# Bias columns, a softmax scaling and two steps of a weight split move to other engines and other places in the queues

## The chip, the cores and the metric

One core of one Trainium2 chip runs the whole program. The metric is device time in microseconds (us); smaller is better. The kernel before took 667.5 us (median of 665.89, 667.50 and 667.67).

## What is computed

An attention block is followed by two gated feed-forward layers, all in 32-bit floats.

```
scores = q @ k.T / 8 + bias      # 2 batches x 8 heads, 576 x 576, head size 64
bias   = relu(x @ w1 + b1) @ w2  # x from the positions alone; 32 hidden units -> 8 heads
attn   = exp(scores - max); attn /= attn.sum() + 1e-9
x      = (attn @ v) as 1152 tokens x 512
x      = (sigmoid(x @ w_gate) * (x @ w_val)) @ w_out           # layer 0, 1536 hidden
xn     = x / rms(x) * g
out    = (silu(xn @ w_gate) * (xn @ w_val)) @ w_out            # layer 1, 1536 hidden
```

## The kernel before, in words

TensorE's fast format holds fewer bits than a 32-bit float, so the feed-forward operands are each a high word plus a low word, and every product is three matmuls. The weights lie in memory as 64-bit floats (two 32-bit words). A *piece* is one 128x512 block of them (72 pieces: 2 layers x 12 hidden blocks x gate, value and output weights). A piece is loaded into one of three buffers `wr` (`piece_load`) and made into a 32-bit float and then into the two words by four steps (`piece_step`), of which the last two are alike in both kernels:

- step 0 masks and shifts the upper word (VectorE, into `tt`);
- step 1 takes the absolute value of the upper word (ScalarE, `ab`), merges sign and shifted bits (VectorE, `ff`), scales the lower word to an integer (ScalarE, `rb`) and adds the two (GpSimd, `ff`);
- step 2 sets tiny values to zero (VectorE, `ab`) and rounds to the high word (ScalarE, `wh` or `wv`);
- step 3 subtracts to get the low word (VectorE, `wl` or `wv`).

The order of every engine's queue is the order in which the program issues, so each engine works strictly through its own list. `advance` deals out piece steps one at a time, in a fixed cycle over the four steps, wherever `ready` allows the next piece to take that step. `fetch` issues the load of a piece two ahead of the count of first merges done (`done[1]`).

The attention part runs in 40 *turns* (one batch, one pair of heads, one block of 128 or 64 query rows each). Each turn issues, in an order written out by hand (`ORDERS`): M0/M1, score plus bias and its minimum (VectorE); X0/X1, exponentials with sums (ScalarE); N, the sums of the turn before inverted (VectorE) and its two 128x576 exponentials scaled (`normal`); T, transposes on TensorE of the block three turns back, and E0 to E2, their copies out of PSUM; Q, the scores of the next turn; P and V, the products with v; and A and b, up to two steps of the bias table (`bias_step`). A bias step builds four 128-wide column tiles `ht` for a new group of 16 positions (`bias_h`), multiplies those of the group before (`bias_mm`, results `be`), and mirrors and stores the one before that (`bias_end`). The first 16 of 36 groups are done before turn 0; groups 16 to 25 fall to turns 0 to 4, two in each; groups 26 to 35 to turns 8 to 17. `BIAS_H` names, for each group, the columns that ScalarE and GpSimd build; VectorE builds the others.

The feed-forward part is 72 steps `s`: a block of 384 tokens times one hidden block. At each, `gate_val(s)` issues 24 matmuls and the gating (ScalarE `sg`, VectorE `g`, ScalarE `gh`), `low_part(s)` the gated rows' low word `gl` (VectorE), and `out_mm(s-2)` the 12 matmuls of the output product of two steps earlier. Output products of two to four hidden blocks gather in a pair of PSUM tiles `acc`; at the last of them (`closing`) the sums are read out into `part` (VectorE, in part ScalarE), and the next group's first matmul may only then overwrite them. Steps of pieces are dealt out between these in two halves, as many as `pace` says (5 to 8).

Of the kernel before, what the change touches and what calls it, by code (L numbers as in the profile page):

```python
# [8 lines left out]
F32 = mybir.dt.float32  # L9
F32R = mybir.dt.float32r  # L10
U32 = mybir.dt.uint32
I32 = mybir.dt.int32
AF = mybir.ActivationFunctionType
ALU = mybir.AluOpType
# [20 lines left out]


BIAS_H = {k: ((), (2, 3) if k % 2 else (3,)) for k in range(16)}
BIAS_H |= {k: ((), (3,)) for k in range(16, 36)}

BIAS_HALF_DVE = (0, 1, 2, 3)  # L40
PRE = 16
# [33 lines left out]
def fused_kernel(ctx: ExitStack, tc: tile.TileContext, qk, vp, tab, pcol, invp, prm, wts, rg, out):  # L75
    nc = tc.nc
# [11 lines left out]
    def bank2(nm):  # L88
        return ps2.tile([128, 2, 512], F32, tag="two", name=nm)
# [206 lines left out]
    def jobs(n):  # L296
        return 1 if UNITS[n][2] == 4 else 2
# [56 lines left out]
    def normal(n):  # L354
        p, sm = st[n, "p"]
        k = jobs(n)
        nc.vector.tensor_scalar(sm[:, :k], sm[:, :k], 1e-9, None, op0=ALU.add)
        rs = w2.tile([128, 2], F32, tag="rs", name=f"rs{n}", bufs=3)
        nc.vector.reciprocal(rs[:, :k], sm[:, :k])  # L359
        for j in range(k):  # L360
            nc.gpsimd.tensor_scalar(p[:, j], p[:, j], rs[:, j : j + 1], 1.0, op0=ALU.mult, op1=ALU.mult)  # L361

    pts = {}

# [63 lines left out]
    def members(l, g):  # L428
        a = sum(GROUPS[l][:g])
        return range(a, a + GROUPS[l][g])  # L430
# [7 lines left out]
    NS = len(STEPS)  # L438
# [5 lines left out]
    wraw = {}  # L444
    mid = {}
# [21 lines left out]
    def piece_step(k, i):  # L467
        mc = pools["mc"]
        if i == 0:
            tt = mc.tile([128, 512], U32, tag="tt", name=f"tt{k}")  # L470
            nc.vector.tensor_scalar(  # L471
                tt, wraw[k][:, :, 1], 3, 0x3FFFFFFF, op0=ALU.logical_shift_left, op1=ALU.bitwise_and
            )
            mid[k] = tt
        elif i == 1:
            raw = wraw.pop(k)
            lw, hw = raw[:, :, 0], raw[:, :, 1]
            tt = mid[k]
            ab = mc.tile([128, 512], F32, tag="ab", name=f"ab{k}", bufs=3)
            nc.scalar.activation(ab, hw.bitcast(F32), AF.Abs)  # L480
            ff = mc.tile([128, 512], U32, tag="ff", name=f"ff{k}", bufs=2)
            nc.vector.scalar_tensor_tensor(ff, hw, 0xC0000000, tt, op0=ALU.bitwise_and, op1=ALU.bitwise_or)  # L482
            rb = mc.tile([128, 512], I32, tag="rb", name=f"rb{k}")
            nc.scalar.activation(rb, lw, AF.Copy, scale=2.0**-29)  # L484
            nc.gpsimd.tensor_tensor(ff.bitcast(I32), ff.bitcast(I32), rb, op=ALU.add)  # L485
            mid[k] = (ab, ff)
        elif i == 2:
            ab, ff = mid[k]
            nc.vector.scalar_tensor_tensor(ab, ab, TINY_HI, ff.bitcast(F32), op0=ALU.is_ge, op1=ALU.mult)  # L489
            nc.scalar.activation(ring[k % RING][0], ab, AF.Copy)  # L490
        else:
            ab, _ = mid.pop(k)
            hi, lo = ring[k % RING]
            nc.vector.tensor_tensor(lo, ab, hi.bitcast(F32), op=ALU.subtract)
            wp[PIECES[k]] = (hi, lo)
# [24 lines left out]
    def low_part(s):  # L520
        gh, g32 = gt[s]
        gl = pools["me"].tile([128, CH], F32R, tag="gl", name=f"gl{s}", bufs=3)
        nc.vector.tensor_tensor(gl, g32, gh.bitcast(F32), op=ALU.subtract)  # L523
        gt[s] = (gh, gl)

    def out_mm(s):
        l, g, c, f = STEPS[s]
        gh, gl = gt.pop(s)
        oh, ol = wp[l, f, 2]
        head, last = f == members(l, g)[0], f == members(l, g)[-1]  # L530
        final = g == len(GROUPS[l]) - 1
        if head:
            acc[c] = (bank2(f"acc{l}{g}{c}a"), bank2(f"acc{l}{g}{c}b"))
        a = acc[c]
        cs = slice(c * CH, c * CH + CH)
        def product(m):
            dst = a[m % 2][:, m // 2, :CH]
            for k, (st_, mv) in enumerate(((oh, gh), (oh, gl), (ol, gh))):
                nc.tensor.matmul(
                    dst, st_[:, m * 128 : m * 128 + 128], mv, start=(head and k == 0), stop=(last and k == 2)  # L540
                )

        def collect(m):
            dst = a[m % 2][:, m // 2, :CH]
            pt = part[m][:, cs]
            if g > 0:
                nc.vector.tensor_tensor(pt, dst, pt, op=ALU.add)  # L547
            elif m % 2:
                nc.vector.tensor_copy(pt, dst)
            else:  # L550
                nc.scalar.activation(pt, dst, AF.Copy)
            if final and l == 1:
                (nc.sync if m % 2 == 0 else nc.scalar).dma_start(out[m * 128 : m * 128 + 128, cs], pt)


        for m in range(NCC):
            product(m)
            if s == NS - 1:
                collect(m)
        if not last:  # L560
            return
        if s < NS - 1:
            for m in range(NCC):
                collect(m)
        if final and l == 0:
            norm_queue.append([s + 2, c, 0, None])
# [52 lines left out]
    done = [0, 0, 0, 0]  # L619
    loaded = [0]  # L620
    phase = [0]

    def released(k):
        return USES[PIECES[k][:2]][-1] + 3
# [4 lines left out]
    def closing(s):  # L629
        return 0 <= s < NS - 1 and STEPS[s][:3] != STEPS[s + 1][:3]  # L630


    def pace(s):
        need, begun = 5, done[0] + done[1] + done[2] - 3 * done[3]
        for k in range(done[3], min(NPC, done[3] + RING)):
            todo = 4 * (k + 1 - done[3]) - begun
            need = max(need, -(-todo // max(1, deadline(k) - s - 1)))
        return min(need, 8)

    def ready(i):  # L640
        k = done[i]
        if k >= (NPC if i == 0 else done[i - 1]):
            return False
        if i == 0:
            return k < loaded[0] and done[1] >= k
        if i == 1:
            return done[2] >= k - 1 and done[3] >= k - 2
        return i == 3 or k < room[0]
# [5 lines left out]
    def fetch():  # L654
        while loaded[0] < NPC and done[1] >= loaded[0] - 2:
            piece_load(loaded[0])
            loaded[0] += 1

    def advance(limit, micro):
        room[0] = limit  # L660
        idle = 0
        while micro and idle < 4:
            fetch()
            i = (2, 1, 0, 3)[phase[0]]
            phase[0] = (phase[0] + 1) % 4
            if ready(i):
                piece_step(done[i], i)
                done[i] += 1
                micro -= 1
                idle = 0  # L670
            else:
                idle += 1
# [18 lines left out]
    for n in range(NU + TL + 1):  # L691
# [13 lines left out]
        def load_new():  # L705
# [16 lines left out]
            "E1": lambda: evac(1),  # L722
            "E2": lambda: evac(2),
            "N": lambda: 0 <= n - 1 < NU and normal(n - 1),
            "C": lambda: n >= NBIAS + LAG and advance(EARLY if live else EARLY + MORE, 1 if live else 2),
            "B": lambda: live and feed_bias(n + 4),
            "A": lambda: nb > 1 and bias_step(),
# [24 lines left out]
    for s in range(EARLY + MORE, RING):  # L752
        tag, size = ("pt", 9 * 128) if s < EARLY + MORE + 2 else ("v", 1024)
# [5 lines left out]
    for s in range(NS + 2):  # L759
        while s < NS and (STEPS[s][0], STEPS[s][3], 1) not in wp:  # L760
            advance(done[3] + 1, 1)
        if 0 < s < NS:
            gate_val(s)
        micro = pace(s)
        if any(q[0] <= s for q in norm_queue):
            micro = min(micro, 2)

        parts = (0, micro) if closing(s - 2) else (micro // 2, micro - micro // 2)
        for half in range(2):
            k = done[3]  # L770
            if k < NPC:
                lim = k
                while lim < NPC and lim < k + 3 and (lim < RING or released(lim - RING) <= s):
                    lim += 1
                advance(lim, parts[half])
            if half == 0:
                if s < NS:
                    low_part(s)
                if s > 1:
                    l, _, _, f = STEPS[s - 2]  # L780
                    while (l, f, 2) not in wp:
                        advance(done[3] + 1, 1)
                    out_mm(s - 2)
                while norm_queue and norm_queue[0][0] <= s:
                    _, c, stage, box = norm_queue.pop(0)
                    norm_stage(c, stage, box)
                    if stage < 3:
                        norm_queue.append([s + 1, c, stage + 1, box])
# [68 lines left out]
```

## Time and profile before

| | us |
|---|---|
| median of three runs | 667.5 |
| the profiled execution's own time | 664.12 |
| its span, first to last instruction | 662.3 |
| TensorE busy | 643.4 (97%) |
| VectorE busy | 454.8 (69%) |
| ScalarE busy | 348.6 (53%) |
| GpSimd busy | 211.6 (32%) |

The profile names engines PE (TensorE matmul), PEld (its weight loads), DVE (VectorE), ACT (ScalarE), POOL (GpSimd) and SP (the queue that issues most DMAs); L12 is line 12 of the kernel. TensorE's granted clock was 0.999 of full speed on average. Turn 0 begins at 28.43 us of the span, and the first feed-forward matmul is at 189.06 us.

### The profile page before, as it was taken

The numbers are of one execution on the slowest core, as the hardware profiler recorded it, in microseconds if no ns is written. First come the engines' busy times: TensorE is split into PE (matmuls) and PEld (weight loads), VectorE is DVE, ScalarE is ACT, GpSimd is POOL, SyncE is SP. The second block draws the span as 40 slices with busy tenths as digits, with TensorE's granted clock in tenths as the row PEclk, the third lists the DMA queues.
The fourth block names the chain that finished last, engine by engine and source line by source line (L and its number), as shares of the span: only waits on it lengthen the run. The fifth ranks groups of instructions, "written<-read, shape, count | busy, mean of one in ns | idle before, by whom it ended". The sixth has DMA issues, their size and how long they took to land.

```text
span 662.3 us, 11825 instructions
## 1 busy us (share of the span) xinstructions
PE 643.4 (97%) x4454; PEld 575.6 (87%) x4454; DVE 454.8 (69%) x968; ACT 348.6 (53%) x743; POOL 211.6 (32%) x259
## 2 busy tenths in 40 slices
PE   8889999999999899999999999999999999999997
PEld 4236666777679899999999999999999999999997
DVE  6997898688656667867677678788777777321322
ACT  4648889798685555444444564553555545211110
POOL 6566677476453322222222221110223223000000
PEclk9999999999999999999999999999999999999999
DMA  8866855663124333323233332111234330000111
GB/s 212 276 234 191 226 185 184 232 215 98 50 66 127 104 120 95 96 97 102 93 112 108 96 95 65 64 55 42 84 108 117 98 105 33 1 0 1 48 48 48
DMA packets 28088, 71.73 MB, mean 108 GB/s; under 512 B 3456, under 2 KB 6528, under 8 KB 28032
## 3 DMA queue, kind: packets, MB, share of 16 engines
q1 hardware_dynamic: 27168, 69.80, 34.2%
q10 hardware_dynamic: 864, 1.18, 0.5%
q8 instruction: 35, 0.57, 0.3%
q14 instruction: 21, 0.17, 0.1%
HBM read 57.72 MB, written 13.25 MB: 107 GB/s over the span
## 4 chain that ended last, share of the span: by engine, by line
PE 61%; DVE 13%; ACT 12%; issue 5%; POOL 5%; POOLq 0%; DVEq 0%
PE gv L509 26%; PE s L310 6%; PE pv L399 6%; PE tp L379 6%; POOL ff L485 4%; DVE ab L489 4%; ACT ab L480 3%; ACT rb L484 3%; PE bps L211 3%; DVE part L547 2%; DVE g L515 2%; ACT sg L513 2%; ACT gh L517 1%; ACT wh L490 1%; DVE tt L471 1%
## 5 line engine op out<-in xcount | busy, mean ns | idle before, releaser
L485 POOL TENSOR_TENSOR ff<-ff,rb 128x512 int32<-128x512 int32 x72 | 96.5, 1341 | 284.5 <-ACT rb L484 216.2
L515 DVE TENSOR_TENSOR g<-gv,sg 128x384 f32<-128x384 f32 x72 | 40.1, 558 | 112.5 <-PE gv L509 66.7
L517 ACT ACTIVATE gh<-g 128x384 fp32r<-128x384 f32 x72 | 37.9, 526 | 76.4 <-DVE g L515 76.4
L509 PE MATMUL gv<-nh,wv 128*128 128x384 f32 x288 | 76.5, 337 | 0.0
L509 PE MATMUL gv<-xh,wh 128*128 128x384 f32 x216 | 73.2, 339 | 0.0
L509 PE MATMUL gv<-xl,wh 128*128 128x384 f32 x216 | 72.9, 337 | 0.0
L509 PE MATMUL gv<-xh,wl 128*128 128x384 f32 x216 | 72.9, 337 | 0.0
L489 DVE SCALAR_TENSOR_TENSOR ab<-ab,ff 128x512 f32<-128x512 f32 x72 | 49.9, 693 | 28.7 <-POOL ff L485 28.7
L361 POOL TENSOR_SCALAR p<-p,rs 128x576 f32<-128x576 f32 x72 | 60.4, 847 | 13.4 <-DVE rs L359 13.1
L490 ACT ACTIVATE wh<-ab 128x512 fp32r<-128x512 f32 x42 | 26.5, 631 | 66.9 <-DVE ab L489 66.8
L328 DVE CUSTOM_DVE_ANT_0 t<-s,bt 128x576 f32<-128x576 f32 x72 | 51.8, 751 | 13.8 <-PE s L310 12.3
L193 DVE TENSOR_SCALAR ht<-w1l,bpc 128x304 f32<-128x304 f32 (+17 forms) x100 | 58.8, 652 | 0.0
L513 ACT ACTIVATE sg<-gv 128x384 f32<-128x384 f32 x72 | 34.5, 479 | 44.9 <-PE gv L509 44.8
L349 ACT ACTIVATE p<-t,mn 128x576 f32<-128x576 f32 x72 | 55.2, 767 | 3.4 <-DVE mn L328 3.3
L310 PE MATMUL s<-raw 64*128 64x288 f32 (+1 forms) x320 | 52.6, 427 | 4.6 <-issue 3.1
L399 PEld LDWEIGHTS pv<-pt,v 128*64 128x64 f32 (+1 forms) x800 | 40.2, 136 | 16.8 <-ACT pt L703 10.2
L523 DVE TENSOR_TENSOR gl<-g,gh 128x384 fp32r<-128x384 f32 x72 | 40.1, 557 | 18.6 <-ACT gh L517 18.6
L509 PEld LDWEIGHTS gv<-nh,wv 128*128 128x128 f32 x288 | 52.4, 188 | 0.0
L399 PE MATMUL pv<-pt,v 128*64 128x128 f32 (+2 forms) x800 | 49.6, 268 | 1.0 <-ACT pt L703 1.0
L490 ACT ACTIVATE wv<-ab 128x512 fp32r<-128x512 f32 x30 | 19.0, 633 | 57.5 <-DVE ab L489 57.4
L482 DVE SCALAR_TENSOR_TENSOR ff<-wr,tt 128x512 uint32<-128x512 uint32 x72 | 49.2, 683 | 0.0
L509 PE MATMUL gv<-nh,wh 128*128 128x384 f32 x144 | 48.7, 338 | 0.0
(356 smaller groups left out, 1588.6 us busy)
## 6 DMA issues: line engine op xcount, KB each, us to landing
wr<-wts SPq DMA_DIRECT2D x72, 512.0 KB, 3.6
bias_d<-be SPq DMA_DIRECT2D x36, 295.5 KB, 3.8
bt<-bias_d SPq DMA_DIRECT2D x16, 576.0 KB, 4.8
raw<-qk SPq DMA_DIRECT2D x16, 288.0 KB, 6.3
v<-vp SPq DMA_DIRECT2D x8, 320.0 KB, 3.6
v<-vp SPq DMA_DIRECT2D x8, 160.0 KB, 4.8
bt<-bias_d SPq DMA_DIRECT2D x8, 144.0 KB, 3.2
out<-part SPq DMA_DIRECT2D x6, 192.0 KB, 1.8
```

Source lines behind the costliest of these rows:

```text
L193: nc.vector.tensor_scalar(ht, src, bpc[:, t : t + 1], 0.0, op0=ALU.add, op1=ALU.max)
L310: nc.tensor.matmul(dst, raw[r, 0, it * 128 : it * 128 + rows_of(it)], raw[r, 1, hf * 288 : hf * 288 + 288], start=True, stop=True,)
L328: nc.vector.tensor_tensor_reduce(t, sp[:, :, :288], bt[:, j].rearrange("p (a c) -> p a c", a=2), -SCALE, 3.0e38, ALU.add, ALU.min, mn[:, j ...
L349: nc.scalar.activation(p[:, j], t.rearrange("p a c -> p (a c)"), AF.Exp, bias=mn[:, j : j + 1], scale=-1.0, accum_out=sm[:, j : j + 1],)
L361: nc.gpsimd.tensor_scalar(p[:, j], p[:, j], rs[:, j : j + 1], 1.0, op0=ALU.mult, op1=ALU.mult)
L399: nc.tensor.matmul(box["ps"][j * 64 : j * 64 + 64, :n], v[:k, 2 * j if it == 4 else j, c, :], pt[:k, c, j * 64 : j * 64 + 64] if it == 4 e ...
L482: nc.vector.scalar_tensor_tensor(ff, hw, 0xC0000000, tt, op0=ALU.bitwise_and, op1=ALU.bitwise_or)
L485: nc.gpsimd.tensor_tensor(ff.bitcast(I32), ff.bitcast(I32), rb, op=ALU.add)
L489: nc.vector.scalar_tensor_tensor(ab, ab, TINY_HI, ff.bitcast(F32), op0=ALU.is_ge, op1=ALU.mult)
L490: nc.scalar.activation(ring[k % RING][0], ab, AF.Copy)
L509: nc.tensor.matmul(ps[:, :CH], wt[:, cs], xt[:, cc, :], start=(k == 0), stop=(k == 11))
L515: nc.vector.tensor_tensor(g32, pss[1][:, :CH], sg, op=ALU.mult)
```

## The change

Four edits:

1. Of bias groups 16 to 25, column 1 is built by ScalarE (Relu with a bias) in place of VectorE, and column 3 by VectorE in place of GpSimd.
2. The scaling of the exponentials of turns 0 to 5 is issued to VectorE in place of GpSimd.
3. In a piece, step 0 now holds the shift (VectorE, straight into `ff`), the absolute value and the scaling of the lower word (both ScalarE, the latter in place into `wr`); step 1 is left with the merge (VectorE, in place) and the add (GpSimd, which reads the lower word from `wr`, every second 32-bit word). The dealing cycle is 0, 2, 1, 3 in place of 2, 1, 0, 3, and step 0 may run one piece ahead of step 1.
4. Where `out_mm(s-2)` closes an accumulation, `low_part(s)` is issued behind it, that is behind the reads of the sums.

```diff
 BIAS_H = {k: ((), (2, 3) if k % 2 else (3,)) for k in range(16)}
-BIAS_H |= {k: ((), (3,)) for k in range(16, 36)}
+BIAS_H |= {k: ((1,), ()) if k < 26 else ((), (3,)) for k in range(16, 36)}
+NORM_DVE = range(6)
...
         for j in range(k):
-            nc.gpsimd.tensor_scalar(p[:, j], p[:, j], rs[:, j : j + 1], 1.0, op0=ALU.mult, op1=ALU.mult)
+            if n in NORM_DVE:
+                nc.vector.tensor_scalar(p[:, j], p[:, j], rs[:, j : j + 1], None, op0=ALU.mult)
+            else:
+                nc.gpsimd.tensor_scalar(p[:, j], p[:, j], rs[:, j : j + 1], 1.0, op0=ALU.mult, op1=ALU.mult)
...
         if i == 0:
-            tt = mc.tile([128, 512], U32, tag="tt", name=f"tt{k}")
-            nc.vector.tensor_scalar(
-                tt, wraw[k][:, :, 1], 3, 0x3FFFFFFF, op0=ALU.logical_shift_left, op1=ALU.bitwise_and
-            )
-            mid[k] = tt
+            raw = wraw[k]
+            lw, hw = raw[:, :, 0], raw[:, :, 1]
+            ff = mc.tile([128, 512], U32, tag="ff", name=f"ff{k}", bufs=3)
+            nc.vector.tensor_scalar(ff, hw, 3, 0x3FFFFFFF, op0=ALU.logical_shift_left, op1=ALU.bitwise_and)
+            ab = mc.tile([128, 512], F32, tag="ab", name=f"ab{k}", bufs=3)
+            nc.scalar.activation(ab, hw.bitcast(F32), AF.Abs)
+            nc.scalar.activation(lw.bitcast(I32), lw, AF.Copy, scale=2.0**-29)
+            mid[k] = (ab, ff)
         elif i == 1:
             raw = wraw.pop(k)
             lw, hw = raw[:, :, 0], raw[:, :, 1]
-            tt = mid[k]
-            ab = mc.tile([128, 512], F32, tag="ab", name=f"ab{k}", bufs=3)
-            nc.scalar.activation(ab, hw.bitcast(F32), AF.Abs)
-            ff = mc.tile([128, 512], U32, tag="ff", name=f"ff{k}", bufs=2)
-            nc.vector.scalar_tensor_tensor(ff, hw, 0xC0000000, tt, op0=ALU.bitwise_and, op1=ALU.bitwise_or)
-            rb = mc.tile([128, 512], I32, tag="rb", name=f"rb{k}")
-            nc.scalar.activation(rb, lw, AF.Copy, scale=2.0**-29)
-            nc.gpsimd.tensor_tensor(ff.bitcast(I32), ff.bitcast(I32), rb, op=ALU.add)
-            mid[k] = (ab, ff)
+            ab, ff = mid[k]
+            nc.vector.scalar_tensor_tensor(ff, hw, 0xC0000000, ff, op0=ALU.bitwise_and, op1=ALU.bitwise_or)
+            nc.gpsimd.tensor_tensor(ff.bitcast(I32), ff.bitcast(I32), lw.bitcast(I32), op=ALU.add)
...
         if i == 0:
-            return k < loaded[0] and done[1] >= k
+            return k < loaded[0] and done[1] >= k - 1 and done[2] >= k - 2 and done[3] >= k - 2
...
-            i = (2, 1, 0, 3)[phase[0]]
+            i = (0, 2, 1, 3)[phase[0]]
...
-                if s < NS:
+                if s < NS and not closing(s - 2):
                     low_part(s)
                 if s > 1:
...
                     out_mm(s - 2)
+                if closing(s - 2):
+                    low_part(s)
```

## Rows read from the trace of the kernel before

**Rows 1.** Window: us, then busy (instructions) of PE, PEld, DVE, ACT, POOL, clock, DMA

```profile
300.00:350.00 50.00, 47.41 (x270) 46.83 (x270) 35.70 (x64) 23.91 (x45) 12.11 (x9) 1.00 0.31 96
```

**Rows 2.** Waits of PE: waiting line, releaser, total us, times, longest us

```profile
PE acc001a L539 <- ACT part L551: 2.0, 1, 2.0
...
PE acc021a L539 <- DVE part L547: 1.3, 1, 1.3
PE acc020a L539 <- DVE part L547: 1.3, 1, 1.3
...
PE pv L399 <- ACT pt L703: 1.0, 2, 0.6
PE ss L587 <- DVE nrm L582: 0.9, 1, 0.9
```

**Rows 3.** Windows of turns 0 to 4, columns as in the first group

```profile
28.43:32.99 4.56, 3.13 (x24) 1.70 (x24) 4.49 (x12) 2.91 (x8) 0.00 (x0) 1.00 1.01 368
32.99:39.70 6.71, 4.52 (x40) 2.04 (x40) 6.14 (x15) 2.79 (x6) 4.14 (x6) 1.00 0.68 221
39.70:45.80 6.10, 5.10 (x35) 2.17 (x36) 5.53 (x15) 2.45 (x6) 3.91 (x6) 1.00 0.53 197
45.80:51.57 5.77, 5.77 (x35) 2.60 (x34) 5.74 (x15) 4.12 (x9) 3.77 (x7) 1.00 0.77 259
51.57:56.79 5.22, 5.22 (x52) 2.97 (x50) 5.12 (x15) 3.85 (x9) 2.88 (x5) 1.00 0.56 176
```

**Rows 4.** Timeline, turns 0 and 2: start, us, instruction, count [idle before <- releaser]

```profile
29.79 2.64 DVE L193 TENSOR_SCALAR ht<-w1l,bpc 128x576 f32<-128x576 f32 x6
...
41.33 1.67 DVE L193 TENSOR_SCALAR ht<-w1l,bpc 128x512 f32<-128x512 f32 x3
41.52 2.09 POOL L361 TENSOR_SCALAR p<-p,rs 128x576 f32<-128x576 f32 x2 [2.12 <-DVE rs L359]
...
43.53 0.55 DVE L220 TENSOR_SCALAR be<-bps,nip,corr 128x264 f32<-128x264 f32 x1 [0.53 <-PE bps L211]
```

**Rows 5.** Groups by line, 28.4 to 56.8 us: count, busy us, mean ns, idle before

```profile
L193 DVE TENSOR_SCALAR ht<-w1l,bpc 128x576 f32<-128x576 f32 (+9 forms) x30 | 17.3, 639 | 0.0
```

**Rows 6.** Groups by line of ACT, whole span

```profile
L349 ACT ACTIVATE p<-t,mn 128x576 f32<-128x576 f32 x72 | 55.2, 767 | 3.4 <-DVE mn L328 3.3
L480 ACT ACTIVATE ab<-wr 128x512 f32<-128x512 f32 x72 | 47.5, 660 | 0.0
L484 ACT ACTIVATE rb<-wr 128x512 int32<-128x512 uint32 x72 | 47.5, 660 | 0.0
...
L490 ACT ACTIVATE wh<-ab 128x512 fp32r<-128x512 f32 x42 | 26.5, 631 | 66.9 <-DVE ab L489 66.8
...
L513 ACT ACT_TABLE_LOAD x2 | 2.6, 1283 | 3.7 <-PE gv L509 3.7
L216 ACT ACT_TABLE_LOAD x1 | 1.3, 1283 | 6.3 <-DVE corr L678 6.3
```

**Rows 7.** Timeline, 302 to 306 us, around a closing

```profile
303.69 0.56 DVE L523 TENSOR_TENSOR gl<-g,gh 128x384 fp32r<-128x384 f32 x1 [0.59 <-ACT gh L517]
...
304.17 0.55 DVE L547 TENSOR_TENSOR part<-acc012a,part 128x384 f32<-128x384 f32 x1
...
305.79 0.41 PE L539 MATMUL acc020a<-gh,wv 128*128 128x384 f32 x1 [1.28 <-DVE part L547]
```

**Rows 8.** Timeline of POOL, 198 to 211 us: first and last of four adds

```profile
198.04 1.28 POOL L485 TENSOR_TENSOR ff<-ff,rb 128x512 int32<-128x512 int32 x1 [1.57 <-ACT rb L484]
...
210.04 1.29 POOL L485 TENSOR_TENSOR ff<-ff,rb 128x512 int32<-128x512 int32 x1 [2.60 <-ACT rb L484]
```

**Rows 9.** The page's groups by line: the other operations of a piece

```profile
L489 DVE SCALAR_TENSOR_TENSOR ab<-ab,ff 128x512 f32<-128x512 f32 x72 | 49.9, 693 | 28.7 <-POOL ff L485 28.7
...
L482 DVE SCALAR_TENSOR_TENSOR ff<-wr,tt 128x512 uint32<-128x512 uint32 x72 | 49.2, 683 | 0.0
```

**Rows 10.** The page's DMA issues: count, KB each, median us to landing

```profile
wr<-wts SPq DMA_DIRECT2D x72, 512.0 KB, 3.6
```

## The prediction

> **What bounds the kernel now.** I read the busy shares first, then the list of waits of TensorE (PE), then windows of the stages, then the timeline where PE idles. PE is busy 643.4 us of a span of 662.3, so only what stops PE can be won: about 19 us, of which the start-up takes a good part. In a mid feed-forward window PE is busy 47.41 of 50 us, with 270 matmuls at the spacing of about 0.174 us that the timeline shows for 384 columns (270 x 0.174 = 47.0), so little stall hides inside "busy" there; VectorE has 35.7, ScalarE 23.9, GpSimd 12.1 [rows 1]. The stops are few: three first matmuls of an output sum wait 2.0, 1.3 and 1.3 us for reads of the sum before (`acc...` <- `part`), two `pv` 1.0 us, `ss` 0.9 us [rows 2]. The other place is turns 1 to 4 of turns 0 to 4 in [rows 3], which take 6.71, 6.10, 5.77 and 5.22 us, with VectorE busy for 6.14, 5.53, 5.74 and 5.12 of them: there VectorE is the bound, and PE's scores wait for its minima.
>
> **Turns 0 to 4: bias columns and scalings.** With GpSimd quiet, six columns take 2.64 us, 0.43 each, in turn 0; beside GpSimd's scalings three narrower ones are at it for 1.67 us [rows 4], and the 30 columns of these turns sum to 17.3 us [rows 5]. Each slows the other: two scalings on GpSimd took 2.09 us in turn 2, against 0.74 each when VectorE did no columns. Scaled by width from 0.43 at 576, the 30 cost 11.5 us alone, so the contention is 5.8 us. The count on VectorE does not change (column 3 comes, column 1 goes). What comes is two scalings a turn in turns 1 to 6, of the columns' kind and width: 0.43 each, bounds 0.43 and 0.85 (double, as when contended), plus some 0.1 of waiting for the inverse: +0.96 a turn.
>
> Turn by turn: turn 0 had no GpSimd work beside its columns, so 0. Turn 1: its columns lose about 1.1 us of contention and gain 0.96, and the idle 0.57 us (6.71 - 6.14) goes in the main, since it was a wait behind GpSimd's column: -0.55. Turn 2: the columns lose 1.09, gain 0.96, and the 0.57 idle, a wait of the `be` read for PE (0.53) [rows 4], is filled by the scalings: -0.6. Turn 3: -0.75 on VectorE, but ScalarE takes over. Its two new columns have no row; nearest are 0.66 (512 from SBUF) and 0.77 (576 with a sum) [rows 6], and I take 0.7: 4.12 + 1.4 = 5.5 us against 5.77 [rows 3], so -0.3. Turn 4: 3.85 + 1.3 = 5.15 on ScalarE, and PE, which has no idle there, needs about 5.2: 0. In turns 5 and 6 two more scalings push E2 and M0 back: +0.15. Sum **-1.3 us**, bounds -3.3 (the busy time alone: 5.8 saved, 3.8 added, 1.3 idle) and +1 (dear scalings, and each new ScalarE column ahead of a `be`). On ScalarE, `be` and X1 queue behind a new column, and the copies of the next transposes wait for those; in turns 1 and 2 it idles ahead of `be` anyway. From turn 5 on the chain of waits runs along PE alone as far as 172 us, so what is won arrives later.
>
> A rule of the Trainium skill speaks against this edit (ScalarE: Activation LUTs, Rules for kernel authors): relu belongs on VectorE, not ScalarE. The rows agree on the price, 0.43 against about 0.7; kept on VectorE the ten columns would add 0.8 us to each of these turns there, and the gain would be near 0.5 instead of 1.3. Which engine is full decides here, and that is VectorE.
>
> **The closers.** At 303.69 `gl` starts, after 0.59 us of idle for `gh`; only behind it come the reads of the closed sum, from 304.17, and PE's next sum starts at 305.79 after 1.28 us of idle [rows 7]. With `gl` behind the reads, they start at once after `g`: 0.59 + 0.47 (from `gl` to the first read) = 1.06 us earlier, which leaves 0.2 of 1.28. The sum's own matmuls were long done. The same holds at 326.18 (1.3 us) and, with ScalarE's half of the reads, at 221.81 (2.0 us). There are 20 closings; the other 17 show no such wait. The edit adds a wait: VectorE stands at a read for PE's last products, up to 2 us (12 matmuls); behind it queue `gl(s)` and piece steps, and `gl(s)` is wanted two steps (some 12 us) later, so nobody waits.
>
> **The piece loop.** Why were the reads late at all? VectorE and ScalarE ran a step behind PE. Four adds on GpSimd, from 198.04 to 210.04, are 4.00 us apart [rows 8], and this is a loop: add 1.3, zeroing 0.69 [rows 9], high word 0.63, absolute value 0.66, lower word 0.66 [rows 6] = 3.94, because in ScalarE's queue the absolute value and scaling of the next piece stand behind the high word of this one, which waits for this add. `sg` and `g` then wait in the same queues. With both in step 0 and the cycle 0, 2, 1, 3, ScalarE does them for the next piece before that high word; the loop is add, zeroing, merge: 1.3 + 0.69 + 0.68 [rows 9] = 2.7 us. At the fastest dealing (8 in a feed-forward step of 36 x 0.174 = 6.26 us, so 3.13 us a piece) the queues no longer fall behind. This takes the 0.2 us left of each closer too: **-4.5 us** for the three, bounds -4.6 and -2 (order alone, and the ScalarE half stays).
>
> No operation is added per piece, but two change form. The scaling writes every second word in place; no row has such a write, and I take 0.66, with 0.66 and 1.3 as bounds. GpSimd reads the lower word at a step of two: 1.3 as now [rows 8], bounds 1.3 and 2.6. At 2.6 the loop is again 4.0 us, as now, and pieces are wanted only about every 6.3 us, so even that costs no more than part of the 0.2 us. `wr` comes free at the end of the add, not of the scaling, 1.3 us later. Its next load lands in 3.6 us [rows 10]; nine steps are dealt between the merge that sets it off and the first use, 7 us at the fastest, against some 2 for merge and add and 3.6 for the load, so nothing queues behind it on SP, and VectorE and ScalarE, whose step 0 would wait for it with `sg` and `g` behind, don't.
>
> **Small stops.** `pv` waited 1.0 us for copies that stood behind a piece's ScalarE work at 196 to 198 us, `ss` 0.9 us for a late VectorE [rows 2]. Which piece step meets them is shuffled; I take -0.4 of 1.9, bounds +0.6 and -1.9.
>
> **Sum.** -1.3 - 4.5 - 0.4 = -6.2 us: the profiled execution's 664.12 becomes 657.9 (span 656.1). That execution lies 3.4 under the median of the runs, so on their scale 667.5 - 6.2 = **661.3 us**.
>
> **Rivals.**
> (a) The closers' stops move instead of going: something else in the queue (a piece's zeroing waiting for an add) holds the reads as long. For it: ScalarE's part of the reads at 221.81 was behind a whole lagging queue. Against it: `gl` is directly ahead of the reads [rows 7]. Then only the turns pay: 667.5 - 1.3 = 666.2, no change that can be told.
> (b) The turns give nothing, ScalarE's columns holding up copies as VectorE's did: 667.5 - 4.9 = 662.6.
> (c) All small stops go with the lag, and turn 3 and 4 pay in full: -2.3 - 4.6 - 1.9 = -8.8, 658.7.
> (d) Slower: Relu forces table loads. The trace has three loads, 1.28 us each [rows 6], and no Relu. If it alternated with Exp's table, the ten columns would cost 20 loads, 25.7 us on ScalarE, which has 16.1 us of work in the 28.4 us of turns 0 to 4 (sums of [rows 3]), plus 7 of columns: 48.8 - 28.4 = +20 us, less 4.9 from the pieces: 683. It decides from about 8 loads on (28.4 - 16.1 - 7.0 = 5.3 us of slack, and 4.9 of gain). Against it: Identity, Copy, Exp and Abs alternate here with no load between them [rows 6].
>
> The Trainium skill (ScalarE: Activation LUTs, Table sets: the hidden batching unit) lists relu and abs as filler in every set, so by it (d) does not happen; the trace agrees for Abs, and no row has Relu.
>
> (e) That the change doesn't do what it says: `ready` or `pace` holds the next step 0 back, and the loop stays at 4.0 us. The closers still get their 1.06 us and perhaps 1 at 221.81: 667.5 - 1.3 - 3.1 = 663.1.
>
> **How the numbers follow.** A measurement of this kernel tells 0.3% (2.0 us) from no change: faster is under 665.5, slower over 669.5. Forecast 60% (658.8 to 663.8 by its bounds), (b) 8%, (c) 8%, (e) 8%, (a) 10%, (d) 2%, and 4% for a slowing that I don't see. Faster: 60 + 8 + 8 + 8 = 84%; same: 10%; slower: 6%. The range of 8 in 10 goes from 657.5 to 665.5: it leaves out (a), (d) and the unseen above, and part of (c) below.
>
> **What would show it.** Right: PE's waits for `part` gone at the three closings; adds in a burst about 2.7 to 3.1 us apart; in turns 1 to 4 columns at 0.34 to 0.43 us each and turns of about 6.2, 5.5, 5.5 and 5.2 us; Relu at about 0.7 with no table load before it; the add at 1.3 to 1.5. Wrong: a new wait of PE for weights or of step 0 for a load of `wr`, turns as long as before with ScalarE full, or an add over 2.6.

## The result, and the profile after

The changed kernel took 656.97 us (median of 655.60 to 658.50), the kernel before 666.69 in the same comparison; the ratio is 0.9868, 95% interval 0.9845 to 0.9891. The forecast was 661.3 in a range of 657.5 to 665.5 against a median before of 667.5. The sign was right and the size too small: 9.7 us by the medians instead of 6.2. The median as it stands lies 0.5 us under the range; put on the forecast's scale by the ratio (0.9868 x 667.5 = 658.7), it lies inside, near the lower end. The profiled execution took 656.51 us, its span is 654.7.

The page's first lines after (part 1, then the chain that ended last): busy us, share of the span, instructions.

```profile
PE 641.9 (98%) x4454; PEld 576.1 (88%) x4454; DVE 486.9 (74%) x980; ACT 354.4 (54%) x753; POOL 209.6 (32%) x237
...
PE 94%; ACT 1%; issue 0%; DVE 0%; DVEq 0%
```

PE's own busy time hardly moved (643.4 to 641.9); the span lost what stood between its matmuls. The chain of waits, of which PE had 61% before, is now PE for 94%. The list of waits of PE after, against [rows 2]:

```profile
PE s L312 <- issue: 2.9, 2, 1.4
PE s L312 <- DVE mn L330: 2.0, 1, 2.0
PE bps L213 <- DVE ht L195: 2.0, 3, 1.0
PE pv L404 <- ACT pt L705: 1.4, 2, 0.9
```

All waits for `part`, and that for `ss`, are gone; `pv` waits 1.4 us where it waited 1.0. Where the 7.6 us of span went is seen by laying the starts of the two traces' `gate_val` matmuls beside each other (worked out from the timelines of PE; after minus before, both from their span's start):

```
start of turn 0 / turn 6     28.43 -> 28.38 (-0.06)    59.59 -> 59.46 (-0.13)
gate_val(1)                 198.43 -> 197.99 (-0.44)
gate_val(5), past acc001a   224.25 -> 221.40 (-2.85)   step -2.41
gate_val(9), past acc010a   249.90 -> 246.55 (-3.35)   step -0.50
gate_val(18), past acc020a  307.96 -> 303.11 (-4.85)   step -1.50
gate_val(21), past acc021a  328.36 -> 321.95 (-6.41)   step -1.56
gate_val(33), past ss       406.33 -> 398.73 (-7.60)   step -1.19
```

The rows `past acc...` stand behind the first matmuls of an output sum, that is behind the closings; the list of waits of before has none for `acc010a`. So turns 0 to 6 gave 0.1 us, where 1.3 was expected, and what follows gave 7.5: 0.3 up to the feed-forward part and 7.2 in it. The windows of turns 0 to 4 after, against [rows 3] (the third number from the end is the granted share of PE's clock):

```profile
28.38:32.92 4.54, 3.13 (x24) 1.71 (x24) 4.50 (x12) 3.75 (x9) 0.22 (x1) 1.00 1.01 357
32.92:39.91 6.99, 5.56 (x40) 2.40 (x40) 6.03 (x17) 4.00 (x8) 0.48 (x2) 0.76 0.70 226
39.91:46.34 6.43, 5.58 (x34) 2.23 (x35) 5.45 (x17) 3.42 (x8) 0.26 (x1) 0.73 0.74 285
46.34:51.44 5.10, 5.10 (x34) 2.44 (x33) 5.03 (x17) 4.53 (x9) 0.59 (x2) 1.00 0.86 284
51.44:56.29 4.85, 4.85 (x49) 3.17 (x53) 4.78 (x17) 4.80 (x11) 0.30 (x1) 1.00 0.59 196
```

Turns 1 and 2 are longer than before (6.99 and 6.43 against 6.71 and 6.10) although VectorE's columns went nearly as forecast, from 17.3 us [rows 5] to 12.3 for the same 30 (11.5 in the forecast). In both of them PE ran part of the time at half its clock, 1.2 GHz:

```profile
35.60:39.00 3.40, 3.40 (x33) 1.38 (x32) 2.51 (x7) 2.19 (x5) 0.23 (x1) 0.50 0.39 89
39.00:42.50 3.50, 2.07 (x16) 1.00 (x8) 3.43 (x11) 1.78 (x4) 0.25 (x1) 0.99 0.99 362
42.50:45.90 3.40, 3.40 (x25) 0.99 (x24) 2.49 (x7) 1.93 (x4) 0.26 (x1) 0.51 0.57 222
```

In the profiled execution of before the same stretches were at 1.00. Ahead of the first fall PE had stood for 2.0 and 1.4 us, ahead of the second for 1.4 us, with scores and bias products between. The length of the stops alone does not tell: before it stood there for 1.5, 1.5 and 1.6 us and kept its clock. The timeline of VectorE in turns 1 and 2 shows what the lower clock does:

```profile
34.66 0.95 DVE L364 TENSOR_SCALAR p<-p,rs 128x576 f32<-128x576 f32 x2
35.53 1.32 DVE L195 TENSOR_SCALAR ht<-w1l,bpc 128x544 f32<-128x544 f32 x3
...
37.74 0.57 DVE L222 TENSOR_SCALAR be<-bps,nip,corr 128x280 f32<-128x280 f32 x1 [0.89 <-PE bps L213]
...
44.71 0.55 DVE L222 TENSOR_SCALAR be<-bps,nip,corr 128x264 f32<-128x264 f32 x1 [0.91 <-PE bps L213]
```

Scalings and columns take about what was forecast (0.47 and 0.44 us each), and then VectorE stands 0.9 us at each of these `be` for bias products that PE computes at half speed; before, it stood 0.53 us there [rows 4].

A closer after (timeline, the closing of [rows 7]): the reads come first, `gl` behind them, and PE's next sum has no idle in front.

```profile
296.51 0.56 DVE L549 TENSOR_TENSOR part<-acc012a,part 128x384 f32<-128x384 f32 x1 [0.96 <-PE acc012a L541]
...
298.43 0.55 DVE L525 TENSOR_TENSOR gl<-g,gh 128x384 fp32r<-128x384 f32 x1
...
301.00 0.34 PE L541 MATMUL acc020a<-gh,wv 128*128 128x384 f32 x1
```

The reads ended 2.5 us before PE wanted the tile, and the first of them waited for PE: at this closing VectorE no longer runs a step behind.

The piece loop is not what was forecast. Adds on GpSimd in the same burst as [rows 8], and VectorE beside one of them:

```profile
196.41 1.29 POOL L488 TENSOR_TENSOR ff<-ff,wr 128x512 int32<-128x512 int32 x1
...
200.15 1.73 POOL L488 TENSOR_TENSOR ff<-ff,wr 128x512 int32<-128x512 int32 x1 [1.72 <-ACT xf L416]
...
204.20 1.54 POOL L488 TENSOR_TENSOR ff<-ff,wr 128x512 int32<-128x512 int32 x1 [1.85 <-ACT ab L480]
207.84 1.51 POOL L488 TENSOR_TENSOR ff<-ff,wr 128x512 int32<-128x512 int32 x1 [2.09 <-ACT wh L492]
```

```profile
200.63 1.54 DVE L478 TENSOR_SCALAR ff<-wr 128x512 uint32<-128x512 uint32 x1
...
202.09 0.81 DVE L491 SCALAR_TENSOR_TENSOR ab<-ab,ff 128x512 f32<-128x512 f32 x1
```

They are 3.6 to 4.1 us apart, not 2.7 to 3.1. The shift on VectorE (0.41 us at best) starts 0.5 us after the add and ends only after it: 1.54 us. Between the adds at 204.20 and 207.84 VectorE does the shift (until 206.03), the gating `g` of a feed-forward step (0.55), the zeroing (0.68) and the merge (0.68), one behind the other. The groups by line show the stretching over the whole span: the add went from 1341 to 1574 ns, the shift from 481 to 863.

```profile
L488 POOL TENSOR_TENSOR ff<-ff,wr 128x512 int32<-128x512 int32 x72 | 113.3, 1574 | 250.8 <-DVE ff L487 130.8
...
L478 DVE TENSOR_SCALAR ff<-wr 128x512 uint32<-128x512 uint32 x72 | 62.1, 863 | 0.0
```

From 188 us on, 39 VectorE operations take over 1.1 us, against 8 before, and each of them ends 0.3 to 0.8 us behind the end of an add that was running when it started. The Trainium skill (GPSIMD Engine Reference, Key points) says that GpSimd shares its SBUF interfaces with VectorE and meets operations in a two-port mode or with two SBUF inputs. The trace agrees for two SBUF inputs: all 23 subtractions of two SBUF tiles (`wl`, `wv`, `gl`) that started during an add were stretched (1.0 to 1.8 us instead of 0.55 to 0.68), and none of the 24 gatings `g` that did, with one input from PSUM (0.55 to 0.56). The shift, with one input, was stretched too, and no row shows its mode. The step of two in the add's input costs next to nothing: its shortest took 1288 ns, against 1267 before.

If the adds come hardly faster, why are the reads no longer late? ScalarE's queue at the first closer shows it, before and then after:

```profile
217.72 0.63 ACT L490 ACTIVATE wh<-ab 128x512 fp32r<-128x512 f32 x1 [2.34 <-DVE ab L489]
218.26 0.65 ACT L480 ACTIVATE ab<-wr 128x512 f32<-128x512 f32 x1
218.81 0.65 ACT L484 ACTIVATE rb<-wr 128x512 int32<-128x512 uint32 x1
219.38 0.48 ACT L513 ACTIVATE sg<-gv 128x384 f32<-128x384 f32 x1
```

```profile
216.24 0.64 ACT L492 ACTIVATE wh<-ab 128x512 fp32r<-128x512 f32 x1 [2.08 <-DVE ab L491]
216.78 0.47 ACT L515 ACTIVATE sg<-gv 128x384 f32<-128x384 f32 x1
```

The gating's `sg` stood behind the two ScalarE operations of the next piece, and those behind a high word that waits for an add; now it stands right behind the high word. From the gate's last matmul to `sg` (worked out from the timelines) went 5.0, 7.6, 8.0 and 8.0 us in steps 1 to 4 before, and 4.2, 6.8, 5.8 and 4.1 after.

### The profile page after: what moved, and what is told of

The parts are those of the page before. It is cut to its first block, busy times and chain, and to the rows that moved or that the text cites. A ratio compares the mean times of both kernels' runs of the same rounds, so it can differ in the third digit from the quotient of the medians.

```text
span 654.7 us, 11794 instructions
## 1 busy us (share of the span) xinstructions
PE 641.9 (98%) x4454; PEld 576.1 (88%) x4454; DVE 486.9 (74%) x980; ACT 354.4 (54%) x753; POOL 209.6 (32%) x237
## 4 chain that ended last, share of the span: by engine, by line
PE 94%; ACT 1%; issue 0%; DVE 0%; DVEq 0%
PE gv L511 46%; PE s L312 7%; PE pv L404 7%; PE tp L384 6%; PE bps L213 4%; PE acc122a L541 1%; PE acc102b L541 1%; PE acc100b L541 1%; PE acc121b L541 1%; PE acc120b L541 1%; PE acc101b L541 1%; PE acc110b L541 1%; PE acc030b L541 1%; PE acc112b L541 1%; PE acc111b L541 1%; PE acc032b L541 1%
## 5 line engine op out<-in xcount | busy, mean ns | idle before, releaser
L488 POOL TENSOR_TENSOR ff<-ff,wr 128x512 int32<-128x512 int32 x72 | 113.3, 1574 | 250.8 <-DVE ff L487 130.8
L478 DVE TENSOR_SCALAR ff<-wr 128x512 uint32<-128x512 uint32 x72 | 62.1, 863 | 0.0
L195 DVE TENSOR_SCALAR ht<-w1l,bpc 128x304 f32<-128x304 f32 (+17 forms) x100 | 53.5, 599 | 0.0
L525 DVE TENSOR_TENSOR gl<-g,gh 128x384 fp32r<-128x384 f32 x72 | 45.3, 629 | 7.0 <-ACT gh L519 7.0
L487 DVE SCALAR_TENSOR_TENSOR ff<-wr,ff 128x512 uint32<-128x512 uint32 x72 | 49.1, 682 | 0.0
L366 POOL TENSOR_SCALAR p<-p,rs 128x576 f32<-128x576 f32 x60 | 48.2, 815 | 1.4 <-DVE rs L361 1.1
```

Of the source, the lines that this page charges most:

```text
L195: nc.vector.tensor_scalar(ht, src, bpc[:, t : t + 1], 0.0, op0=ALU.add, op1=ALU.max)
L478: nc.vector.tensor_scalar(ff, hw, 3, 0x3FFFFFFF, op0=ALU.logical_shift_left, op1=ALU.bitwise_and)
L487: nc.vector.scalar_tensor_tensor(ff, hw, 0xC0000000, ff, op0=ALU.bitwise_and, op1=ALU.bitwise_or)
L488: nc.gpsimd.tensor_tensor(ff.bitcast(I32), ff.bitcast(I32), lw.bitcast(I32), op=ALU.add)
```

## The experiments

Every execution has its mean granted clock besides its time, and that is what makes the times readable. Of the 50 executions of the kernel before that were taken beside the experiments, two were at 0.999 (663.95 and 664.21 us), one at 0.997 (664.91), the others at 0.985 to 0.995 and 664.7 to 669.4 us. A straight line through all executions of all kernels, one offset for each kernel, has a slope of 0.36 us for each 0.001 of clock, with 0.6 us left over. The last column is each kernel's value on it at 0.999 (worked out, not measured, and uncertain by 0.2 to 0.4 us). The medians of before are those of the three comparisons in which the experiments were taken (that of the changed kernel had 666.69), and each ratio is an estimate with its own interval, not the quotient of two medians. loop_turns_fill, content_fill, norm_fill and bias_fill ran on another chip than the other experiments; the line puts before 0.2 us lower there.

| kernel | median us | ratio to before (95%) | clock of its executions | at 0.999 |
|---|---|---|---|---|
| before | 666.57, 666.98, 666.06 | | 0.985 to 0.999 | 663.9 |
| changed | 656.97 | 0.9868 (0.9845 to 0.9891) | 0.991 to 0.997 | 654.9 |
| turns_only (edits 1, 2) | 666.13 | 0.9983 (0.9965 to 1.0) | 0.987 to 0.997 | 662.5 |
| order_only (edit 4) | 662.16 | 0.9934 (0.9916 to 0.9953) | 0.987 to 0.995 | 659.7 |
| loop_only (edit 3) | 656.77 | 0.9858 (0.9836 to 0.9881) | 0.994 to 0.999 | 656.7 |
| loop_order (3, 4) | 660.55 | 0.9912 (0.9892 to 0.9931) | 0.986 to 0.992 | 657.0 |
| loop_turns (1, 2, 3) | 659.64 | 0.9901 (0.9875 to 0.9926) | 0.986 to 0.992 | 656.1 |
| cycle_only | 664.80 | 0.9969 (0.9952 to 0.9986) | 0.991 to 1.0 | 662.6 |
| fill (changed + 18 matmuls) | 655.31 | 0.9840 (0.9814 to 0.9866) | 0.997 to 1.0 | 655.4 |
| fill_before (before + 18) | 664.45 | 0.9965 (0.9952 to 0.9978) | 0.997 to 1.0 | 664.3 |
| loop_turns_fill (1, 2, 3 + 18) | 655.69 | 0.9843 (0.9824 to 0.9863) | 0.997 to 1.0 | 655.3 |
| content_fill | 658.44 | 0.9886 (0.9868 to 0.9904) | 0.997 to 0.999 | 658.4 |
| norm_fill (2 + 18) | 663.01 | 0.9951 (0.9935 to 0.9967) | 0.997 to 0.999 | 662.6 |
| bias_fill (1 + 18) | 662.28 | 0.9941 (0.9925 to 0.9958) | 0.995 to 0.999 | 661.7 |

**The four edits apart.** turns_only is the kernel before with edits 1 and 2, order_only with edit 4, loop_only with edit 3; loop_order is the changed kernel with edits 1 and 2 undone. Their diffs are those hunks of the change.

turns_only. 

> Kernel before with edits 1 and 2 alone (bias columns and scalings). Theory (the turns' gain is eaten by TensorE's clock): the granted clock falls to half in two stretches of turns 1 and 2 as in the changed kernel, turn 6 starts about 0.1 us earlier than before, time 0 to -0.5 us. Rival (VectorE and ScalarE are simply as full as before, the clock plays no part): the same time, but also where the clock stays at full in the profile; the columns' PE reads then show no stretching.

Measured 666.13, 0.4 under before. Its profile shows the clock at 0.57 and 0.69 in turns 0 and 1 (not 1 and 2), at 1.00 in turn 2, and at 0.57 again after PE's 2.0 us stop at the first closer. So the theory holds in the main; that the loss was larger than in the changed kernel's profile (turn 6 starts 1.6 us later than before, not 0.1 earlier) shows that where the clock falls differs between executions.

```profile
28.60:35.07 6.47, 5.04 (x24) 2.29 (x24) 4.49 (x12) 3.84 (x8) 0.22 (x1) 0.57 1.02 369
35.07:42.66 7.59, 5.40 (x40) 2.86 (x40) 6.04 (x18) 3.94 (x8) 0.36 (x2) 0.69 0.71 233
...
224.00:228.00 4.00, 4.00 (x15) 3.77 (x14) 2.82 (x7) 2.14 (x4) 0.41 (x1) 0.57 0.06 24
```

order_only. 

> Kernel before with edit 4 alone (low rows behind the closed sum's reads). Theory (order and loop are both needed): the reads start 1.06 us earlier, so PE's stops at the three closings shrink from 2.0, 1.3 and 1.3 to about 1.0, 0.2 and 0.2: -3.2 us. Rival (the order does it all): the three stops go, -4.6 us. Other rival (the lag of the queues decides, not the order): 0 to -1 us.

Measured 662.16, 4.4 under before, which is more than the theory's 3.2 and close to the rival's 4.6, but not as either had it. The list of PE's waits has the first closer unchanged and the other two gone, and `ss` with them:

```profile
PE acc001a L539 <- ACT part L551: 2.1, 1, 2.1
PE bps L211 <- DVE ht L193: 2.0, 3, 1.1
PE pv L399 <- ACT pt L703: 1.0, 2, 0.6
```

At the first closer the lag of the queues decides, at the others the place of `gl` is enough.

loop_only. 

> Kernel before with edit 3 alone (piece steps). Theory: the gating of the closing step comes about 2 us earlier, so the first stop (2.0) shrinks to about 0.9 and the other two (1.3) go or shrink to 0.3, and the wait for ss (0.9) goes: -3 to -4.5 us. Rival (the order does it all): under -1.2 us, only ss. Adds some 3.6 to 4.0 us apart at 196 to 208 us, as in the changed kernel, with VectorE operations of over 1.5 us beside them.

Measured 656.77, better than the most that was expected (9.8 us by the medians, 7.2 at equal clock): all the closers' waits are gone although `gl` is still ahead of the reads. Its list of PE's waits has no `part`:

```profile
PE s L310 <- issue: 3.1, 2, 1.6
PE bps L211 <- DVE ht L193: 1.8, 3, 0.9
PE s L310 <- DVE mn L328: 1.5, 1, 1.5
PE pv L399 <- ACT pt L700: 1.4, 2, 0.9
```

Three of its four executions had the clock at 0.999.

loop_order. 

> Changed kernel with edits 1 and 2 undone (bias columns and scalings as before). Theory: the whole gain of the feed-forward part, -7.5 us, and the clock stays at full through turns 0 to 4; turn 6 starts 0.1 us later than in the changed kernel: time within 0.5 us of the changed kernel (about -9 of the before median's scale). Rival (the turns' edits do pay and the profiled execution hides it): 1.3 us slower than the changed kernel.

Measured 660.55, which looks as if the order cost 3.8 us on top of the loop. But its executions all had the clock at 0.986 to 0.992; at equal clock, by the line, it is 657.0 against 656.7. Neither theory foresaw that the clock would fall in a kernel whose turns are those of before, and in its profile it also fell once after a stop of `pv` near 197 us. The comparison with the changed kernel at equal clock (654.9) speaks for the rival's point, that the turns' edits do pay.

**Is it the clock?** fill adds to the changed kernel, and fill_before to the kernel before:

```diff
+FILL = {0: 6, 1: 6, 2: 6}
...
+        if n in FILL:
+            fb = bank(f"fill{n}")
+            for _ in range(FILL[n]):
+                nc.tensor.matmul(fb[:, :128], ones, ones, start=True, stop=True)
         for x in ORDERS[0 if n < NBIAS else 1 if live else 2].split():
```

fill. 

> Changed kernel plus six matmuls of ones (into a PSUM tile that nothing reads) at the start of each of turns 0, 1 and 2, where TensorE idles for the minima. Theory (the turns' gain is lost to TensorE's clock): the granted clock stays at 1.0 through turns 1 to 3, the executions show 0.997 to 0.999, turn 6 starts 1.3 to 2 us earlier than in the kernel before at full clock, median 654.5 to 655.5. Rival (the clock plays no part): no earlier turns, and the 18 added matmuls cost 0 to +3 us: 657 to 660.

Measured 655.31, all five executions at 0.997 to 1.0. The windows of turns 1 to 4 of its profile, 6.06, 5.45, 5.07 and 4.87 us at full clock:

```profile
33.21:39.27 6.06, 6.06 (x58) 3.96 (x57) 5.99 (x17) 3.95 (x8) 0.36 (x3) 1.00 0.70 200
39.27:44.72 5.45, 5.21 (x43) 2.70 (x42) 5.38 (x17) 3.56 (x8) 0.39 (x2) 1.00 0.98 375
44.72:49.79 5.07, 4.93 (x32) 2.12 (x29) 5.00 (x17) 4.26 (x8) 0.73 (x2) 1.00 0.87 287
49.79:54.66 4.87, 4.87 (x50) 3.21 (x53) 4.80 (x17) 4.84 (x11) 0.53 (x2) 1.00 0.66 219
```

From the start of turn 0 to that of turn 6 it takes 29.14 us, against 31.16 before and 31.17 in fill_before's profile: the edits are worth 2.0 us there once PE keeps its clock, and the 18 matmuls themselves cost no time there.

fill_before. 

> Kernel before plus the same 18 matmuls. Theory: the clock stays at full in more executions, and the median goes from 666.6 to about 664.2 (the executions of before at 0.999). Rival: they only cost, 666.6 to 669.

Measured 664.45, all twelve executions at 0.997 or more, against 3 of 50 without. So 18 matmuls that nothing reads save 2.5 us (ratio 0.9965), and the falling clock was a cost of the kernel before too, one that its profiled execution happened not to have.

**Is the order needed beside the loop?** loop_turns undoes edit 4 alone; loop_turns_fill holds the clock as well.

loop_turns. 

> Changed kernel with edit 4 undone (low rows in their old place). Theory (with the new piece steps the order adds nothing): within 0.3 us of the changed kernel once both are taken at the same granted clock, no wait of TensorE for a closed sum's reads; the median may differ by 1 to 2 us with the clock. Rival (both are needed with the turns' edits): a stop of 0.5 to 1 us at the first closing.

Measured 659.64, at clocks of 0.986 to 0.992. Its profile has no wait for `part`. At 0.991 and 0.992 it took 658.06 and 658.68 us, the changed kernel at 0.991 657.43 and 658.50; that is level, but too few executions to tell 0.3 us, and by the line it is 1.2 slower at equal clock. With the clock held the comparison is cleaner:

loop_turns_fill. 

> Changed kernel with edit 4 undone, plus the 18 matmuls of ones that hold the clock. Theory (with the new piece steps the order of the low rows adds nothing): the time of the changed kernel with these matmuls, 655.3 within 0.4 us, no wait of TensorE for a closed sum's reads. Rival (the order still pays 1 us or more at the closers): 656.3 or more.

Measured 655.69 against fill's 655.31 (ratios 0.9843 and 0.9840, each about 0.002 to 0.003 either way): beside the loop the order adds nothing that can be told, and the 1 us of the rival doesn't show.

**What in edit 3 does it?** cycle_only keeps the two ScalarE operations in step 1, content_fill keeps the old cycle.

```diff
 # cycle_only: step 0 holds the shift alone; step 1:
+            nc.scalar.activation(ab, hw.bitcast(F32), AF.Abs)
+            nc.scalar.activation(lw.bitcast(I32), lw, AF.Copy, scale=2.0**-29)
             nc.vector.scalar_tensor_tensor(ff, hw, 0xC0000000, ff, op0=ALU.bitwise_and, op1=ALU.bitwise_or)
 # content_fill: the new steps, with
-            i = (0, 2, 1, 3)[phase[0]]
+            i = (2, 1, 0, 3)[phase[0]]
```

cycle_only. 

> Kernel before with the new dealing cycle (0, 2, 1, 3), the new readiness and the shift in place, but with the absolute value and the scaling of the lower word still in step 1. Theory (ScalarE's two operations behind the high word make the loop): adds in a burst stay 3.9 to 4.0 us apart, the closers' stops stay, 663.8 at full clock, 664 to 667 as measured. Rival (the dealing order brings it): the time of the kernel with edit 3 alone, 656.8.

Measured 664.80. The median is in the theory's range, but the cycle is worth something: its two executions at full clock took 661.44 and 662.16 us, where 663.8 was expected, and at equal clock it is 1.3 under before. The adds of a burst stay 4.1 us apart, behind ScalarE:

```profile
201.97 1.29 POOL L484 TENSOR_TENSOR ff<-ff,wr 128x512 int32<-128x512 int32 x1 [1.57 <-ACT wr L481]
...
206.04 1.31 POOL L484 TENSOR_TENSOR ff<-ff,wr 128x512 int32<-128x512 int32 x1 [2.48 <-ACT xf L411]
...
210.10 1.32 POOL L484 TENSOR_TENSOR ff<-ff,wr 128x512 int32<-128x512 int32 x1 [2.47 <-ACT wr L481]
```

PE still waits 2.1, 1.0 and 0.6 us at the closers, and `sg` stands behind the two ScalarE operations in steps 3 and 4, as before.

content_fill. 

> Kernel before plus the 18 matmuls, with the two ScalarE operations and the shift in step 0 and the merge in step 1 as in the changed kernel, but in the old dealing cycle (2, 1, 0, 3) and with the old readiness. Theory (what stands behind the high word in ScalarE's queue makes the loop, not the cycle): 657 to 658, the time of edit 3 alone (656.7) plus the matmuls, closers' stops gone. Rival (both are needed): 660 to 664.5.

Measured 658.44, 6.0 under fill_before and 0.4 over the range of the theory: the place of the two ScalarE operations carries most of edit 3. No wait for `part` is left. As in the changed kernel and in loop_only, `sg` of step 3 stands right behind a high word. Against loop_only it lacks about 1.7 us at equal clock; what its profile shows there is the seam between attention and feed-forward, where `pv` waits four times, 2.8 us in all, and the clock falls once after it:

```profile
PE pv L400 <- ACT pt L701: 2.8, 4, 0.9
```

**The two edits of the turns.** norm_fill and bias_fill are fill_before with edit 2 and with edit 1.

norm_fill. 

> Kernel before plus the 18 matmuls and edit 2 alone (scalings of turns 0 to 5 on VectorE, bias columns as before). Theory (what pays is that VectorE's columns no longer meet GpSimd's): most of the contention goes, as GpSimd keeps one column a step: -0.5 to -1.2 us against the kernel before with the matmuls (664.4): 663.2 to 663.9. Rival (VectorE's added 0.96 us a turn weighs more): 664.5 to 667.

Measured 663.01, 1.4 under fill_before and a little more than expected.

bias_fill. 

> Kernel before plus the 18 matmuls and edit 1 alone (bias columns off GpSimd, scalings still there). Theory: the columns still meet GpSimd's scalings, but TensorE no longer waits for GpSimd's column behind them (0.57 and 1.05 us in turns 1 and 2): -0.5 to -1.2 us against 664.4: 663.2 to 663.9. Rival (ScalarE's columns hold up the copies): 664.4 to 666.

Measured 662.28, 2.2 under fill_before, more than expected. No execution of these two overlaps with those of fill_before (664.01 to 665.06), but the two can't be told apart by their times (662.22 to 663.45, 661.66 to 663.47). In the profiles turns 0 to 6 shorten by 1.3 us with edit 2 and by 2.0 with edit 1, and by 2.0 with both (fill): beside edit 1, edit 2 gave nothing there. VectorE's time doesn't explain this: the 30 columns take 17.4 us in fill_before, 12.9 with edit 2, 15.0 with edit 1 and 12.3 with both. What edit 1 has beyond is that PE no longer waits for a column of GpSimd; that this makes the difference is argued, not shown.

## Why the prediction was right, and where not

**What bounds the kernel**: right as far as it went. PE's stops could be won, and the chain is PE's now; PE's clock could be won too, and the prediction has no term for it.

**The closers, -4.5: measured -6.0** (2.41 + 0.50 + 1.50 + 1.56). The stops went as forecast. The term was too small for two reasons. A stop of PE costs more between starts of matmuls than the idle that the list of waits prints: at the first closer 2.33 us pass from the start of the last matmul to that of the next, where 0.17 is normal, against 1.99 printed. And a smaller loss behind the closing at 247 us (0.50) was under the list's view. The order's share was wrong: alone it takes two closers whole and leaves the first at 2.1, where the forecast took 1.06 us off each, and with edit 3 it gives nothing.

**The piece loop**: the culprit was right (ScalarE's two operations behind the high word; cycle_only and content_fill tell it apart from the cycle), the way in which it cost time was not. "The loop is add, zeroing, merge: 2.7 us" left out VectorE's other operations, the shift stretched by the add and the gating; adds went from 4.0 us apart to 3.8 on average. So "the queues no longer fall behind" was wrong too: from step 1 to step 2 the lag of `sg` grew by 2.6 us, as before. What the rows show in its place is the order in ScalarE's queue: `sg` no longer has the two operations in front of it (1.1 us of the 2.6 that it came earlier at the first closer). There it started at 216.78 instead of 219.38, with its step's matmuls from 208.65 instead of 209.09, and that was enough. In the profiles that keep the stop (before, order_only, cycle_only) the two operations stand directly ahead of `sg` of step 3, in those of edit 3's content (after, loop_only, content_fill) they don't. So the stops went as forecast by another way than the one forecast, and in that the prediction had luck.

**Turns 0 to 6, -1.3: measured -0.1 in the profiled execution and -2.0 at full clock.** The step that failed is "Turn 1: ... -0.55. Turn 2: ... -0.6": it took PE at the clock that the trace of before showed. With the clock held (fill) turns 1 and 2 came to 6.06 and 5.45 us (forecast 6.2 and 5.5). Turns 3 and 4, at 5.07 and 4.87 (forecast 5.5 and 5.2), were too careful: in turn 3 ScalarE with 4.26 us did not take over, and in turn 4 it was full, but with 4.84 us instead of 5.15.

**Small stops, -0.4**: `ss` went whole (-1.2), `pv` grew by 0.4, so about -1.5 with the seam.

**The sum against the runs.** "That execution lies 3.4 under the median" was read as an offset to carry along. It was the clock: the profiled execution was one of the few in which it held. For the changed kernel the profiled execution lies 0.5 under its median. With the clock held on both sides the change is worth 664.45 - 655.31 = 9.1 us, near the sum of what the traces show (6.0 + 2.0 + 1.5 = 9.5). The range doesn't follow from its terms as written: added end to end, their bounds give 657.7 to 667.1, not 658.8 to 663.8, and the prediction doesn't say how it got there.

**Rivals.** (d) did not come: Relu took 0.63 to 0.76 us, and the trace has the same three table loads as before. (a) did not come: no new wait took the closers' place. Of (e) the premise came, adds still 3.6 to 4.1 us apart, but not the consequence. Of (b) the outcome came in the profiled execution, turns that give nothing, but not the cause: with the clock held ScalarE's columns pay 2.0 us there (bias_fill). (c), all small stops and the turns in full, 658.7, was the nearest.

It stays open why the clock held in three of loop_only's four executions and in hardly any of before's, though both issue the same instructions up to turn 22. What the runs show is only that matmuls in the idle places hold it.

## What to carry to other kernels

Ask what stands ahead of a wanted operation in its engine's queue, not which engine is busiest: two operations moved away from behind one that waits took 6 us (content_fill) from a kernel whose PE was 97% busy. Where a profile of before shows a clock or a time that most executions do not have, look at the others' first, and size a gain at both clocks. Where TensorE has short stops in an opening stage, try a few matmuls that nothing reads in them: here they were worth 2.5 us to the kernel before, and the edits to that stage 2.0.

## What was not expected of the hardware

In the profiled execution of the changed kernel the granted clock fell to half behind stops of PE of only 1.4 to 2.0 us, and most executions of most of these kernels have a mean clock that points to the same. 18 matmuls of 128 columns held it: the mean is 0.997 or more in 38 of 39 executions of the six kernels that have them, and in 10 of 100 of the others, three of these loop_only's. A shift or a subtraction of SBUF tiles on VectorE that starts while a GpSimd add runs ends only behind it: up to 1.8 us instead of 0.4 to 0.7 (one operation of another kind took 2.07 instead of 0.95). The best kernel here is the changed one with those matmuls, 655.31 us (ratio to before 0.9840, 0.9814 to 0.9866).
